# Where in the load order of the second batch's short chunk its single row stands

## The chip, the cores and the metric

The kernel runs on one core of one Trainium2 chip. The metric is the device time of one execution in microseconds; the time of a kernel is the median of its runs. A profiled execution has a time of its own and, inside it, a span, from the first to the last recorded instruction. All positions below ("at 62.1 us") are counted from the start of that span. The engines are PE (matmul), DVE (vector), ACT (scalar), POOL (general purpose) and SP, which here only issues DMAs.

## The reference

```python
X = np.fft.fft(x, axis=1); X = np.fft.fft(X, axis=2); h = X.real       # x: 8 x 3008 x 256, float32
g = h.reshape(24064, 256) @ w_gate                                      # 256 -> 1536
val = h.reshape(24064, 256) @ w_val
out = (g / (1 + exp(-g)) * val) @ w_out                                 # 1536 -> 256
```

For each of eight batches the real part of a two-dimensional Fourier transform is taken over 3008 rows and 256 columns, and a SwiGLU block is applied to each row of it.

## The kernel before

**Transform.** The input rows of a batch are folded by symmetry on POOL (a row with its mirror row, a column with its mirror column), then multiplied on PE with tables of cosines and sines that are made on the chip in the first microseconds. Of the 188 pairs of rows of a folded quarter, 128 form the "long chunk" (tile `XA`, all 128 partitions) and 60 (`NCR`) the "short chunk" (tile `XC`, partitions 0 to 59 or 64 to 123). Row 0 of each quarter has no partner: it is the single row, four rows of 1 KB, put on the partition behind the short chunk (60 or 124).

**The SwiGLU block.** The columns are cut into 24 tiles of up to 512 columns (`wide`); a tile has 12 units of 128 hidden features, so there are 288 units `(t, f)`. A unit makes `g` and `v` on PE (L1336) for the rows and the mirrored rows at once; ACT takes the SiLU (L1448, L1520, L1523), DVE the products (L1539, L1550), and POOL the product of two mirrored units, `hm` (L1547). The pair's operands lie in `sv`, which has two buffers. PE then multiplies `hp` and `hm` with `w_out` (L1598), ACT copies the result out of PSUM (L1604), and SP stores it (L1610). The transform of the next batch (fold on POOL, products at L1756 on PE, sums into `Pt` and `Qt` at L1773 on DVE) runs in between.

**Order.** The first batch's transform and the weights' first part are written out by hand (up to L682). From there all work is recorded as operations with an engine, an estimated duration, reads and writes (`S.add`), and a list scheduler (`Sched.run`) puts them into a fixed order for each engine. For DMAs it models SP's time (`us`), the landing (`lat`) and a shared ring (`ring`). A change of such a number can therefore change the order on every engine. At run time each engine works through its own list in order, waiting on semaphores.

**The loads in question.** `load_c(b)` lists the DMAs of the short chunk: `mid`, the single row (L160); `ups`, 15 DMAs of 32 KB into four partitions each (L158, the rising rows); and the falling sets (L163). For batch 1 the falling sets are split in two halves of four DMAs of 60 KB (`downs[0]`, `downs[1]`, L167), and between the halves a copy inside `XC` (L171) moves one half of the rising rows from partitions 64 to 123 to partitions 0 to 59. `run_loads` hands these DMAs to the scheduler, four to a unit; `k` is the position in the list, and `r` names the earlier positions that the copy reads. Behind them in SP's order come the long chunk of batch 1 (`load_a`: 16 rising DMAs at L148, 4 falling ones of 256 KB at L150), the first stores (L1610), and batch 2's short chunk.

Before all of these SP issues two fills of zeros (L660), 64 KB each, into partitions 60 to 63 and 124 to 127 of `XC`. The single row of batch 1 goes to partition 124, so it has to come after the second fill; the rising and falling rows don't touch those partitions. POOL issues three loads of weights in this time: gate and value columns into `XA` (L387, 512 KB each, at 14.4 and 15.2 us) and `w_out` (L1970, 768 KB, at 24.2 us).

DMAs that SP and ACT issue take eight completion semaphores in turn, so a DMA is issued only when the one eight places earlier has landed.

POOL's list around 62 us reads: `hm` (L1547), `hp` (L1556), the first fold of the long chunk of batch 1 (`SDf<-XA`, L180, and L181), which waits for all of `load_a(1)`, and then `hm` again.

Of the kernel before, what the change touches and what calls it, by code (L numbers as in the profile page):

```python
# [31 lines left out]
def kernel(  # L32
# [33 lines left out]
    NCR = GH - P  # L66
# [50 lines left out]
    XC = const.tile([P, 8, 2, D], F32, name="XC")  # L117
# [14 lines left out]
    LC, NC_ = 4, NCR // 4  # L132

    def up_block(b, j, n):
        return rows_at(b, 2 * j - 1, [[2 * D, n], [R * D, 4], [1, 2 * D]])

    def rows_at(b, row, ap):
        return bass.AP(tensor=x.tensor, offset=(b * M + row) * D, ap=ap)

    def down_set(b, a, j, L, n):  # L140

        return rows_at(b, R * (a + 1) - 2 * j, [[2 * L * D, n], [-2 * D, L], [1, 2 * D]])
# [9 lines left out]
    def load_c(b, q):  # L152

        X3 = XC.rearrange("p a q d -> p a (q d)")
        p0 = 64 * (b % 2)
        pm = p0 + NCR
        r = slice(p0, p0 + NCR)
        ups = [lambda h=h: q.dma_start(out=X3[p0 + LC * h:p0 + LC * (h + 1), 0:4, :],  # L158
                                       in_=up_block(b, JC - LC * h, LC)) for h in range(NC_)]
        mid = [lambda: q.dma_start(out=XC[pm:pm + 1, 0:4, 1],  # L160
                                   in_=rows_at(b, 0, [[R * D, 1], [R * D, 4], [1, D]]))]
        if b != 1:
            return ups + [lambda a=a: q.dma_start(out=X3[r, 4 + a, :], in_=down_set(b, a, JC, LC, NC_))  # L163
                          for a in range(4)] + mid

        def down(a, k):
            q.dma_start(out=XC[0:NCR, 4 + a, 0] if k else XC[r, 4 + a, 0],  # L167
                        in_=rows_at(b, R * (a + 1) - 2 * JC + k, [[2 * LC * D, NC_], [-2 * D, LC], [1, D]]))

        downs = [[lambda a=a, k=k: down(a, k) for a in range(4)] for k in range(2)]  # L170
        return mid + ups + downs[0] + [lambda: q.dma_start(out=XC[0:NCR, 0:4, 1], in_=XC[r, 0:4, 0])] + downs[1]  # L171

    def fold_steps(eng, X, CE, BB, q, r):
        tt = eng.tensor_tensor
# [74 lines left out]
    q = nc.sync  # L249
# [129 lines left out]
    def load_w(first, only=(0, 1)):  # L379
        for i, src in ((0, moe_w_gate), (1, moe_w_val)):  # L380
# [5 lines left out]
            else:  # L386
# [12 lines left out]
                        in_=rows_at(0, 0, [[2 * R * D, 2], [R * D, 2], [1, D]]))  # L399
# [259 lines left out]
    for hi in range(2):  # L659
        q.dma_start(out=X3c[64 * hi + NCR:64 * hi + 64, :].rearrange("p (c d) -> p c d", d=D),  # L660
                    in_=zeros[64 * hi + NCR:64 * hi + 64].unsqueeze(1).to_broadcast([64 - NCR, 16, D]))
# [997 lines left out]
    def run_loads(n):  # L1659
        for what, k, fn in loads[:n]:  # L1660
            up = k < (NA if what[0] == "A" else NC_)
            r, w, us, ring = [], [((what[0],), k)], 0.4 if up else 0.62, 0.57 if up or what[0] == "C" else 1.14
            if what == ("A", 1):
                r = [(("C",), NC_ + 9)]
                us, ring = 0.6, 0.6 if up else 0.9
            if what == ("C", 1):
                us, ring = (0.6, 0.6) if k <= NC_ else (0.9, 0.9)
                if k == NC_ + 5:
                    r = [(("C",), j) for j in range(1, NC_ + 1)]
            S.add("SP", us, fn, r=r, w=w, after=[(("A",), "pre" if k > 15 else "preW")] if what == ("A", 1) else [],  # L1670
                  lat=2.5, ring=ring)
        del loads[:n]
# [4 lines left out]
    def fold_step(what, i, unit):  # L1677
        kind, b = what
        q, j = (1, i) if what == ("C", 1) else divmod(i, 6)
        if i == 0:  # L1680
            run_loads(max((k + 1 for k, (w_, _, _) in enumerate(loads) if w_ == what), default=0))
# [27 lines left out]
    def load_next(what):  # L1709
        kind, b = what  # L1710
        if kind == "A":
            if b + 1 < B:
                loads.extend((("A", b + 1), k, fn) for k, fn in enumerate(load_a(b + 1, nc.sync)))
        else:
            b = b // 2 * 2 + 2
            if b < B:
                loads.extend((("C", b), k, fn) for k, fn in enumerate(load_c(b, nc.sync) + load_c(b + 1, nc.sync)))
# [228 lines left out]
    for i, u in enumerate(units):  # L1946
# [4 lines left out]
        if i == 1:  # L1951
            loads.extend((("C", 1), k, fn) for k, fn in enumerate(load_c(1, nc.sync)))
        if i == A1_LOAD:
            loads[0:0] = ((("A", 1), k, fn) for k, fn in enumerate(load_a(1, nc.sync)))
        run_loads(LOADS if i < 20 else LOADS_LATER)
        if i in ROW_PE:
            row_op(ROW_PE[i])
# [7 lines left out]
        if i == RESCALE:  # L1965
            state["scaled"] = True
            S.add("ACT", 1.3, lambda: nc.scalar.activation(Wm[:, 1], Wm[:, 1], AF.Copy, scale=-0.5),
                  r=[(("Wm",), (fc, 1)) for fc in range(3)], w=[(("Wm",), 1)])
# [58 lines left out]
```

## Time and profile before

| | |
|---|---|
| time, median of 3 runs | 607.42 us (605.87 to 609.76) |
| time of the profiled execution | 608.12 us |
| its span | 606.3 us |
| mean granted TensorE clock | 0.997 |
| busy share of the span: PE, DVE, ACT, POOL | 98%, 94%, 93%, 84% |
| data moved by DMA | 57.65 MB, 95 GB/s on average |

A busy share is an average over the whole span; PE's matmuls are pipelined, so that its busy time counts overlaps once. Waits are inferred from semaphores: a wait for several of them is put down to the one that came last, and sometimes to a neighbour of it.

### The profile page before, as it was taken

Reading aid. Unit: us, or ns where it says so; the run is one execution under the profiler, and the core shown is the slowest. Engines: PE = TensorE matmul, PEld = TensorE weight load, DVE = VectorE, ACT = ScalarE, POOL = GpSimd, SP = SyncE. Lnnn points to the kernel's source line nnn. Section 1 sums busy time; section 2 is a strip of 40 time slices with the busy share of each in tenths; the row PEclk is TensorE's granted clock in tenths of the full one; section 3 lists DMA queues with packets and bytes.
Section 4 is the critical chain, followed back from the end, with each engine's and each line's share of the span. In section 5 each row is a group of like instructions: output and inputs, shape, how many; then the busy total and the mean of one; then the engine's idle time right before and its main releaser. Section 6 shows DMA issues by size and latency. Waiting matters only on the chain.

```text
span 606.3 us, 12501 instructions
## 1 busy us (share of the span) xinstructions
PE 592.3 (98%) x3974; PEld 391.8 (65%) x4031; DVE 572.3 (94%) x1055; ACT 562.1 (93%) x1086; POOL 509.7 (84%) x460
## 2 busy tenths in 40 slices
PE   8999799999999999999999999999999999999997
PEld 5456566666666666666666666666666666666686
DVE  8989799999999999999999999999999999999993
ACT  8899797899989899999999999999999999999994
POOL 8717999999899999998999988888878467687772
PEclk9999899999999999999999999999999999999999
DMA  9837347354725514454234212037211112111112
GB/s 240 124 99 136 113 125 158 104 135 115 159 71 114 129 53 124 119 134 123 62 100 120 70 45 81 18 87 186 63 62 37 55 45 62 45 54 51 54 53 78
DMA packets 50554, 57.65 MB, mean 95 GB/s; under 512 B 7267, under 2 KB 37399, under 8 KB 50489
## 3 DMA queue, kind: packets, MB, share of 16 engines
q1 hardware_dynamic: 47529, 53.97, 33.4%
q0 software_dynamic: 2672, 2.36, 2.6%
q8 instruction: 31, 0.51, 0.3%
q10 hardware_dynamic: 288, 0.52, 0.3%
q14 instruction: 34, 0.28, 0.2%
HBM read 29.43 MB, written 24.65 MB: 89 GB/s over the span
## 4 chain that ended last, share of the span: by engine, by line
PE 82%; DMA 6%; DVE 4%; SPq 2%; ACT 2%; issue 2%; POOL 1%; ACTq 0%; DVEq 0%
PE o L1598 37%; PE g L1336 22%; PE v L1336 18%; DMA XC<-in_x_dram 2%; PE g L1756 2%; DMA XA<-in_x_dram 2%; PE o L1756 2%; DMA XC<-Af 1%; DVE sv L1539 1%; SPq L167 1%; DMA out_dram<-ev 1%; PE v L1598 1%; DVE hp L1550 1%; POOL EOA L502 0%; DVE SA L444 0%
## 5 line engine op out<-in xcount | busy, mean ns | idle before, releaser
L1547 POOL TENSOR_TENSOR hm<-sv 128x1024 bf16<-128x1024 f32 (+2 forms) x137 | 254.9, 1862 | 51.1 <-ACT sv L1523 23.2
L1539 DVE SCALAR_TENSOR_TENSOR sv<-es,v 128x512 f32<-128x512 f32 (+2 forms) x264 | 175.6, 669 | 9.5 <-PE v L1336 4.5
L1598 PE MATMUL o<-Wo,hm 128*128 128x256 bf16 (+1 forms) x1128 | 164.6, 273 | 0.5
L1550 DVE TENSOR_TENSOR hp<-sp,v 128x512 bf16<-128x512 f32 (+2 forms) x238 | 157.7, 670 | 4.7 <-PE v L1336 3.8
L1598 PE MATMUL o<-Wo,hp 128*128 128x256 bf16 (+1 forms) x1104 | 159.9, 272 | 0.7
L1598 PEld LDWEIGHTS <-hm 128*128 128x128 bf16 (+2 forms) x1140 | 112.2, 99 | 59.4 <-issue 3.3
L1598 PEld LDWEIGHTS <-hp 128*128 128x128 bf16 (+2 forms) x1140 | 111.9, 98 | 54.6 <-issue 1.8
L1523 ACT ACTIVATE sv<-g 128x512 f32<-128x512 f32 (+2 forms) x182 | 121.3, 681 | 6.2 <-POOL hm L1547 3.1
L1448 ACT ACTIVATE sp<-g 128x512 f32<-128x512 f32 (+2 forms) x182 | 113.2, 626 | 6.3 <-PE g L1336 3.8
L1336 PE MATMUL g<-Pt,Wp 128*128 128x512 bf16 (+2 forms) x281 | 105.4, 375 | 4.0 <-ACT sv L1523 2.9
L1409 ACT ACTIVATE v<-bc,w 128x512 f32<-128x512 bf16 (+2 forms) x146 | 105.7, 726 | 2.0 <-DVE sv L1539 1.0
L1336 PE MATMUL v<-Pt,Wp 128*128 128x512 bf16 (+2 forms) x287 | 105.3, 375 | 0.4
L1471 ACT ACTIVATE es<-v 128x512 f32<-128x512 f32 (+2 forms) x146 | 90.7, 623 | 5.9 <-DVE sv L1539 3.2
L1473 DVE SCALAR_TENSOR_TENSOR es<-bc,w,v 128x512 f32<-128x512 bf16 (+2 forms) x128 | 93.2, 732 | 2.8 <-PE v L1336 0.4
L1336 PE MATMUL g<-Qt,Wq 128*128 128x512 bf16 (+2 forms) x249 | 91.5, 375 | 0.4
L1336 PEld LDWEIGHTS <-Wp 128*128 128x128 bf16 x576 | 56.3, 98 | 26.7 <-issue 1.6
L1336 PE MATMUL g<-Qt,Wm 128*128 128x512 bf16 (+2 forms) x192 | 72.1, 377 | 0.4
L1452 DVE SCALAR_TENSOR_TENSOR sg<-bc,w,g 128x512 f32<-128x512 bf16 (+2 forms) x92 | 66.1, 721 | 1.4 <-PE g L1336 1.0
L1523 ACT ACTIVATE sv<-sg 128x512 f32<-128x512 f32 (+2 forms) x92 | 64.0, 699 | 1.0 <-DVE sg L1516 0.9
L1336 PEld LDWEIGHTS <-Wq 128*128 128x128 bf16 x430 | 42.0, 98 | 31.5 <-issue 7.1
L1520 ACT ACTIVATE sp<-g 128x512 f32<-128x512 f32 (+2 forms) x92 | 56.9, 619 | 5.5 <-DVE sg L1516 5.1
L1516 DVE SCALAR_TENSOR_TENSOR sg<-sg,g 128x512 f32<-128x512 f32 (+2 forms) x92 | 60.7, 660 | 0.3 <-PE g L1336 0.2
(196 smaller groups left out, 769.9 us busy)
## 6 DMA issues: line engine op xcount, KB each, us to landing
out_dram<-ev SPq DMA_DIRECT2D x96, 128.0 KB
XA<-in_x_dram SPq DMA_DIRECT2D x30, 256.0 KB
XA<-in_x_dram SPq DMA_DIRECT2D x112, 64.0 KB
XC<-in_x_dram SPq DMA_DIRECT2D x28, 120.0 KB
XC<-in_x_dram SPq DMA_DIRECT2D x105, 32.0 KB
bc<-br SPq DMA_DIRECT2D x19, 128.0 KB
St<-Fc SPq DMA_DIRECT2D x12, 128.5 KB
out_dram<-ev SPq DMA_DIRECT2D x12, 120.0 KB
```

Source lines behind the costliest of these rows:

```text
L1336: nc.tensor.matmul(ps[:, :n], Wt[:, gv, fs], src[:, :n], start=start, stop=stop, skip_group_check=True)
L1409: nc.scalar.activation(T_[kv][:, :w], bc[t][:, :w], AF.Copy, scale=w0[:, 1, f:f + 1])
L1448: nc.scalar.activation(sp_to()[:, :w], T_[kg][:, :w], AF.Silu)
L1452: nc.vector.scalar_tensor_tensor(T_[keg][:, :w], bc[t][:, :w], w0[:, 0, f:f + 1], T_[kg][:, :w], op0=Alu.mult, op1=Alu.add)
L1471: nc.scalar.activation(T_[kes][:, :w], T_[kv][:, :w], AF.Copy, scale=2.0 if on_pool(u) > 1 else 1.0)
L1473: nc.vector.scalar_tensor_tensor(T_[kes][:, :w], bc[t][:, :w], w0[:, 1, f:f + 1], T_[kv][:, :w], op0=Alu.mult, op1=Alu.add)
L1516: nc.vector.scalar_tensor_tensor(T_[kgm][:, :w], T_[keg][:, :w], 2.0, T_[kg][:, :w], op0=Alu.mult, op1=Alu.subtract)
L1523: nc.scalar.activation(sv()[:, f % 2, w - 1::-1, 1], T_[kgm if by_dve else kg][:, :w], AF.Silu)
L1539: nc.vector.scalar_tensor_tensor(sv()[:, f % 2, w - 1::-1, 0], T_[kes][:, :w], 2.0, T_[kv][:, :w], op0=Alu.mult, op1=Alu.subtract)
L1547: nc.gpsimd.tensor_tensor(hts_(t)[1][:, f - 1:f + 1, :w], sv()[:, :, :w, 1], sv()[:, :, :w, 0], op=Alu.mult)
L1550: nc.vector.tensor_tensor(hts_(t)[0][:, f, :wp], T_[ksp][:, :wp], T_[kv][:, :wp], op=Alu.mult)
L1598: nc.tensor.matmul(st["ps"][:n, j, :], hts[t][minus][:, f, c:c + n], Wo[:, f, :], start=(f == 0), stop=(f == nF - 1))
```

## The change

The DMA of the single row of batch 1 moves from the head of the list to the place behind `downs[0]`, directly ahead of the copy. The list keeps 25 DMAs. In `run_loads` the numbers follow: the rising rows are now positions 0 to 14, and the single row, now position 19, gets the scheduler's costs of the falling sets (0.9 us) in place of those of the rising rows (0.6 us).

```diff
-        return mid + ups + downs[0] + [lambda: q.dma_start(out=XC[0:NCR, 0:4, 1], in_=XC[r, 0:4, 0])] + downs[1]
+        return ups + downs[0] + mid + [lambda: q.dma_start(out=XC[0:NCR, 0:4, 1], in_=XC[r, 0:4, 0])] + downs[1]
...
             if what == ("C", 1):
-                us, ring = (0.6, 0.6) if k <= NC_ else (0.9, 0.9)
+                us, ring = (0.6, 0.6) if k < NC_ else (0.9, 0.9)
                 if k == NC_ + 5:
-                    r = [(("C",), j) for j in range(1, NC_ + 1)]
+                    r = [(("C",), j) for j in range(NC_)]
```

In the compiled order, the lists of all engines are the same up to the place that runs at about 66 us before the change. There one pair changes places on DVE (`hp`, L1550, now ahead of `sv`, L1539). From about 82 to 160 us neighbouring instructions change places on PE (219 places of its list), DVE (32), ACT (26) and POOL (8), and one pair on SP; behind 160 us the lists are the same again. The number of instructions stays.

## The prediction

> **What bounds the kernel now.** I read the busy shares first. PE is busy nearly all the time, so time is lost only where PE stands still or its clock drops.
>
> ```profile
> PE 592.3 (98%) x3974; PEld 391.8 (65%) x4031; DVE 572.3 (94%) x1055; ACT 562.1 (93%) x1086; POOL 509.7 (84%) x460
> ```
>
> Next came busy time by stretches, to find where PE stands still (columns: stretch, length, busy time of PE, PEld, DVE, ACT, POOL with counts, granted clock, DMA share, GB/s).
>
> ```profile
> 64.20:67.20 3.00, 0.06 (x2) 0.04 (x1) 0.73 (x2) 0.64 (x1) 3.00 (x4) 0.91 0.45 140
> 67.20:70.60 3.40, 3.40 (x14) 2.01 (x14) 3.29 (x6) 3.24 (x7) 3.40 (x4) 0.58 0.40 106
> ...
> 76.00:160.00 84.00, 82.86 (x562) 55.24 (x567) 80.71 (x153) 74.43 (x147) 82.28 (x80) 1.00 0.49 127
> ```
>
> PE is empty for 3 us at 64.2, and the next 3.4 us run at a mean clock of 0.58, which costs another 3.4 x 0.42 = 1.4 us. From 76 to 160 us it lacks 1.1 us in all. The waits between 62 and 76 us say who is behind the hole:
>
> ```profile
> POOL SDf L180 <- DMA out_dram<-ev: 5.1, 1, 5.1
> DVE sv L1539 <- POOL hm L1547: 4.0, 1, 4.0
> ...
> ACT sv L1523 <- POOL hm L1547: 3.1, 1, 3.1
> PE g L1336 <- ACT sv L1523: 2.9, 1, 2.9
> ```
>
> POOL's fold waits 5.1 us, `hm` stands behind it, ACT and DVE need the `sv` buffer that `hm` frees, and PE needs the `g` bank that ACT frees. The fold's releaser is named as a store, but the fold waits for the loads into `XA`; the store was merely issued behind them. POOL's list confirms the order:
>
> ```profile
> 62.08 2.35 POOL L180 TENSOR_TENSOR SDf<-XA 128x1020 f32<-128x1020 f32 x1 [5.05 <-DMA out_dram<-ev]
> 64.39 0.21 POOL L181 TENSOR_TENSOR EOf<-XA 128x4 f32<-128x4 f32 x1
> 64.54 1.89 POOL L1547 TENSOR_TENSOR hm<-sv 128x1024 bf16<-128x1024 f32 x1
> ```
>
> So these loads set the hole, and what is issued ahead of them on SP matters:
>
> ```profile
> 16.58 1.49 SPq L660 DMA_DIRECT2D XC<-Af  x2
> 26.11 0.64 SPq L160 DMA_DIRECT2D XC<-in_x_dram  x1
> 26.80 8.16 SPq L158 DMA_DIRECT2D XC<-in_x_dram  x15
> 35.16 3.62 SPq L167 DMA_DIRECT2D XC<-in_x_dram  x4
> 38.97 0.89 SPq L171 DMA_DIRECT2D XC<-XC  x1
> 39.90 3.49 SPq L167 DMA_DIRECT2D XC<-in_x_dram  x4
> 43.56 0.68 SPq L148 DMA_DIRECT2D XA<-in_x_dram  x2
> ```
>
> SP stands for 8.0 us (18.1 to 26.1) until the second zero fill has landed, because the single row writes the same partition. From 35.2 us on it issues without a pause until the `XA` loads begin at 43.56.
>
> **The change, part by part.**
>
> *The wait.* The rising rows don't touch the filled partitions, so SP may issue them at 18.1 us. But DMAs take eight semaphores in turn: the first six rising rows find theirs free, the seventh needs the first fill's, the eighth the second fill's. Thus six of 15 are issued by 20.3 us (0.34 us each, the spacing of L148), the seventh after the first fill, the eighth at 26.1 as the single row was. The 8 us wait mostly moves to the seventh and eighth rising row. All 25 DMAs remain.
>
> *What the early six gain.* The view of DMA queues in two stretches (q1 is SP's queue, q0 POOL's) decides:
>
> ```profile
> q0 software_dynamic: 394, 0.77, 105.3%
> ...
> q0 software_dynamic: 1257, 0.64, 120.2%
> ```
>
> The first is 16.6 to 20.8 us, the second 26.0 to 30.2 us. In neither did one packet of q1 start, though the fills (issued 16.6) and then the single row and seven rising rows (issued 26.1 to 29.0) were waiting: POOL's weight loads, then `w_out`, kept SP's queue out. Between them the fills drain until about 25.2 us. So the early rows, queued behind the fills, have some 0.8 us before `w_out` starts at 26.0. Their pace: the single row landed at 31.06 (the next issue on its semaphore is at 31.08) and the eighth rising row at 35.15 (which released L167 at 35.16), so 4.09 / 8 = 0.51 us a row. That is 0.8 / 0.51, hence one to two rows done, and one more takes the single row's first turn at 30.2: two to three rows, 1.0 to 1.5 us. I take 1.3. The first falling set, which waits for the eighth rising row, goes out at 33.9 instead of 35.16. Bounds: nothing gets through early (0), or the early rows run beside `w_out` (below, 3.3).
>
> The Trainium skill, page "DMA: Bandwidth & Descriptors", section "Queues, rings and completion order", says that a DMA engine goes round between queues, a packet of at most 64 descriptors at a time. Taken as a fair share this speaks for the larger gain; the trace, with no q1 packet in 4.2 us twice, shows a far coarser turn. By the rule the first falling set would go out near 31.9, by the rows at 33.9.
>
> *The single row in its new place.* It stands between the fourth falling set and the copy: 0.64 us plus a gap of 0.05, 0.69 us, now in the stretch where SP issues without pause. Behind it are the copy, four falling sets, and all loads into `XA`. Before, it lay ahead of them too, but there the rows' landings, not SP, set the pace. Its own waits are over by then. Net: 1.3 - 0.7 = 0.6 us earlier for the `XA` loads (43.0).
>
> *On to PE.* The loads move as a block, so the fold starts at 61.5 and `hm` at 63.9; the hole shrinks from 2.9 to 2.3 us. No drop of the clock followed the 0.8 us that PE stood at 10.4, one followed 2.9 us; 2.3 is nearer to the latter, so I leave the 1.4 us in. Gain 0.6. Nothing is gained beyond POOL's lead: it is busy without a pause from 62.1 to 93.9 us, and PE's transform at 91.08 uses a fold that ends at 90.44, 0.6 us of slack.
>
> The Trainium skill, page "TensorE: Matmul & The Clock Gate", section "Part 1: The HAM clock gate", puts the fall at an idle window of about 3.4 us; here 2.9 us was enough. By that rule 2.3 us would not lower the clock, and the sum would be up to 0.6 us better, what POOL's slack allows.
>
> *The scheduler.* The single row's cost in the model rises by 0.3 us, and the lists between 82 and 160 us change. The swap at 66 us is harmless: `hp` may run in the hole. The others have no price in the trace. From below: the one PE wait between 76 and 160 us, 0.66 us at 145.8 (PE for ACT), goes away. From above: a hole like the one at 64 us with its slow clock, 2.9 + 1.4 = 4.3. Since the swapped instructions are neighbours, I price them by the 0.66 us row, half a chance of one more: +0.3.
>
> *Sum.* -0.6 + 0.3 = -0.3 us on the profiled execution (608.12, span 606.3). It lies 0.7 above the median, 607.42; I apply the difference to the median: 607.1.
>
> **The rivals.**
>
> *A, the early rows run beside `w_out`.* With half of the engines' time from 26.0, 1.6 rows are through by then, 5.1 more by 31.2, the eighth at 31.9: 3.3 us earlier, 2.6 after the single row's cost. The hole and the slow clock vanish, but POOL's lead of 2.6 plus at most 0.6 of slack caps the gain: 3.0, so 604.4. For it: between 20.8 and 23 us both queues had packets (128 and 46). Against: the two empty stretches.
>
> *B, the single row now costs its 0.69 us.* If the fills drain later because the early rows crowd them, no row gets through before `w_out`, and the `XA` loads, the fold and PE's hole move out by 0.7: 608.1. It decides when less than 1.4 rows are through by 26.0. For it: the fills' slow drain (the DMA share from 23.0 to 26.1 is 0.14). This is slower, though within 1%.
>
> *C, the new order opens a hole.* One between 82 and 160 us costs 4.3 as at 64 us, two 8.6: 611.4 to 616. Against: the swaps are small. For: PE there has only 1.1 us to lose and the other engines are at 89 to 98%, so a late buffer is not absorbed. It decides from some 3 us of lateness.
>
> *D, the change does nothing:* SP waits for the fills anyway at the seventh row. It is the forecast with 0 in place of 0.6 and shares its chance.
>
> **How the numbers follow.** Forecast (with D) 0.52, A 0.22, B 0.13, C 0.13. Its own range is 606.0 to 608.0. For the whole, low is the full removal of the hole and clock loss (607.4 - 4.3 = 603.1), a little lower for the scatter of a median; high takes in B and part of C: 602.8 to 610.3. A measurement of this kernel can tell about 1%, 6 us, from no change. Over 1% faster needs more than the hole holds, so only A with scatter: 0.05. Over 1% slower needs two holes of C or one very long: 0.10. The rest, 0.85, lies within.
>
> **What would show it.** Six L158 issues from 18.1, a wait of SP at the seventh and eighth until about 26.1, L167 near 33.9, L160 behind four of them, the first L148 at 43.0, POOL's L180 at 61.5, PE's hole at 64 near 2.3 us. I am wrong if L148 starts before 41.5 (A) or after 43.6 (B), or if PE waits over 2 us between 82 and 160 us (C).

## The result and the profile after

The changed kernel takes 604.2 us (median of 9 runs, 603.54 to 605.0), the kernel before, timed beside it, 608.3 us (9 runs, 605.82 to 611.05): a ratio of 0.9931, 95% interval 0.9909 to 0.9954. That is 0.7% faster. The profiled execution took 604.29 us with a span of 602.4 us (before 608.12 and 606.3). Single executions of one kernel lie up to 8 us apart here, so verdicts go by timed medians, and a profile is one draw. The page's busy shares of the changed kernel look as before:

```profile
PE 591.5 (98%) x3974; PEld 392.1 (65%) x4031; DVE 572.8 (95%) x1055; ACT 562.6 (93%) x1086; POOL 509.4 (85%) x460
```

PE's busy time falls by only 0.8 us, though the span is 3.9 us shorter. The stretches around 64 us tell more (stretch, length, busy time of PE, PEld, DVE, ACT, POOL with counts, granted clock, DMA share, GB/s):

```profile
63.50:66.50 3.00, 2.46 (x17) 1.54 (x16) 2.50 (x4) 2.47 (x5) 3.00 (x3) 1.00 0.41 115
66.50:70.00 3.50, 3.44 (x25) 2.18 (x23) 3.50 (x7) 3.50 (x9) 3.50 (x4) 1.00 0.56 155
76.00:160.00 84.00, 82.86 (x560) 55.14 (x566) 81.29 (x153) 75.59 (x148) 82.17 (x78) 1.00 0.50 132
```

The hole of 2.9 us is down to 0.5, and no stretch at half clock follows: the clock is 1.00 where it was 0.58. These two are the gain: 2.4 us of hole and 1.4 us of slow clock, 3.8 of the 3.9 us. From 76 to 160 us PE is busy for 82.86 us, to the hundredth as before, although its list changed there. The waits from 50 to 90 us of the changed kernel show the same chain as before, each link shorter:

```profile
POOL SDf L180 <- DMA out_dram<-ev: 4.5, 1, 4.5
...
DVE sv L1539 <- POOL hm L1547: 1.0, 1, 1.0
ACT sv L1523 <- POOL hm L1547: 0.7, 1, 0.7
...
PE g L1336 <- ACT sv L1523: 0.5, 1, 0.5
```

POOL's own list of the changed kernel puts the fold 2.6 us earlier (62.08 before), and `hm` too (64.54 before):

```profile
59.49 2.35 POOL L180 TENSOR_TENSOR SDf<-XA 128x1020 f32<-128x1020 f32 x1 [4.51 <-DMA out_dram<-ev]
61.81 0.20 POOL L181 TENSOR_TENSOR EOf<-XA 128x4 f32<-128x4 f32 x1
61.97 1.89 POOL L1547 TENSOR_TENSOR hm<-sv 128x1024 bf16<-128x1024 f32 x1
```

SP's issues in the changed kernel say where it comes from:

```profile
16.62 1.49 SPq L660 DMA_DIRECT2D XC<-Af  x2
18.15 11.56 SPq L158 DMA_DIRECT2D XC<-in_x_dram  x15
32.20 3.61 SPq L167 DMA_DIRECT2D XC<-in_x_dram  x4
35.86 0.65 SPq L160 DMA_DIRECT2D XC<-in_x_dram  x1
36.62 0.89 SPq L171 DMA_DIRECT2D XC<-XC  x1
37.55 3.94 SPq L167 DMA_DIRECT2D XC<-in_x_dram  x4
41.67 2.38 SPq L148 DMA_DIRECT2D XA<-in_x_dram  x7
```

The 15th rising row has been issued by 29.71. With eight semaphores in turn that needs the seventh row landed: so seven rows are in `XC` before 29.7 us, where before the first of them landed only after 31 us. The first falling set goes out 2.96 us earlier (32.20 for 35.16), the loads into `XA` 1.89 us earlier (41.67 for 43.56). The difference is the single row (0.76 us from its issue to the copy's) and 0.46 us more for the second falling half, less 0.15 in the first half.

In the DMA queues of the changed kernel from 26.0 to 30.2 us (packets, MB, share of 16 engines), SP's queue is no longer absent:

```profile
q0 software_dynamic: 1201, 0.61, 115.3%
q1 hardware_dynamic: 100, 0.16, 11.5%
```

Of these 100 packets 89 start between 26 and 28 us, beside `w_out`. SP's queue (q1) from 24 to 26 us and then POOL's (q0) from 26 to 28 us in the kernel before, where SP's has no packet in that second stretch:

```profile
q1 hardware_dynamic: 28, 0.03, 7.7%
q0 software_dynamic: 426, 0.22, 94.6%
```

SP's queue from 24 to 26 us and both queues from 26 to 28 us in the changed kernel:

```profile
q1 hardware_dynamic: 73, 0.10, 27.0%
q0 software_dynamic: 376, 0.19, 87.3%
q1 hardware_dynamic: 89, 0.15, 20.9%
```

### The profile page after: what moved, and what is told of

Its sections match the earlier page's. It is cut to its first block, busy times and chain, and to the rows that moved or that the text cites. A ratio compares the mean times of both kernels' runs of the same rounds, so it can differ in the third digit from the quotient of the medians.

```text
span 602.4 us, 12497 instructions
## 1 busy us (share of the span) xinstructions
PE 591.5 (98%) x3974; PEld 392.1 (65%) x4031; DVE 572.8 (95%) x1055; ACT 562.6 (93%) x1086; POOL 509.4 (85%) x460
## 4 chain that ended last, share of the span: by engine, by line
PE 81%; DMA 6%; DVE 4%; ACT 3%; POOL 2%; issue 2%; SPq 2%; POOLq 0%; ACTq 0%; DVEq 0%
PE o L1598 36%; PE g L1336 22%; PE v L1336 18%; PE g L1756 2%; DMA XC<-in_x_dram 2%; PE o L1756 2%; DMA XC<-Af 2%; DVE sv L1539 1%; DMA XA<-in_x_dram 1%; SPq L167 1%; DMA out_dram<-ev 1%; PE v L1598 1%; DVE hp L1550 1%; ACT sp L1448 1%; ACT v L1409 1%
## 5 line engine op out<-in xcount | busy, mean ns | idle before, releaser
L1539 DVE SCALAR_TENSOR_TENSOR sv<-es,v 128x512 f32<-128x512 f32 (+2 forms) x264 | 176.1, 672 | 5.9 <-PE v L1336 4.2
L1550 DVE TENSOR_TENSOR hp<-sp,v 128x512 bf16<-128x512 f32 (+2 forms) x238 | 158.1, 672 | 4.4 <-PE v L1336 3.8
```

Source lines behind the costliest of these rows:

```text
L1539: nc.vector.scalar_tensor_tensor(sv()[:, f % 2, w - 1::-1, 0], T_[kes][:, :w], 2.0, T_[kv][:, :w], op0=Alu.mult, op1=Alu.subtract)
L1550: nc.vector.tensor_tensor(hts_(t)[0][:, f, :wp], T_[ksp][:, :wp], T_[kv][:, :wp], op=Alu.mult)
```

## The experiments

The theory: SP's rows get through before `w_out` only if they are queued ahead of it; this brings the `XA` loads, and so POOL's fold, forward until PE hardly waits. The first rival: the gain is due to the new lists between 66 and 160 us. The second: `w_out` alone, as the block, sets the start of the `XA` loads. The kernel before was timed beside each group of four experiments, each group on another chip; its medians were 607.55 (35 runs, first four kernels), 609.33 (35, next four) and 609.38 us (26, last four). The ratios below compare with these runs.

**The loads and the lists apart.** The changed DMA order with the old cost for the single row, which gives the old lists on all computing engines:

```diff
-                us, ring = (0.6, 0.6) if k < NC_ else (0.9, 0.9)
+                us, ring = (0.6, 0.6) if k < NC_ or k == NC_ + 4 else (0.9, 0.9)
```

> The loads stand as in the change, but the scheduler's cost of the single row is put back to 0.6 us, so that the lists of PE, DVE, ACT and POOL are those of before, place by place. Theory 1 (the early rising rows let the loads into XA begin earlier, PE's hole at 64 us and the slow clock behind it go): time ratio to before 0.992 to 0.995, first L148 near 41.7 us, hole below 0.8 us, no half clock. Theory 2 (the new order of the compute lists brings the gain): ratio 0.998 to 1.002.

Measured: 605.49 us, ratio 0.9968 [0.9946, 0.9990], between the ranges of the two theories. The first L148 came at 41.53 us as expected, but the profile has a hole of 2.9 us with half clock, which theory 1 had excluded. Run again with the last group:

> The first experiment once more (early rows, lists of before), to tell its 0.9968 from the 0.9931 and 0.9941 of the changed kernel. Theory 1 (the early rows alone bring it all): ratio 0.992 to 0.9955. Theory 2 (the lists bring a part, once the rows are early): ratio 0.9955 to 0.999.

Measured: 606.77 us, 0.9960 [0.9934, 0.9986], in the range of theory 2, though the interval reaches into that of theory 1. The old DMA order with the new cost, hence the new lists:

```diff
-                us, ring = (0.6, 0.6) if k <= NC_ else (0.9, 0.9)
+                us, ring = (0.6, 0.6) if 0 < k <= NC_ else (0.9, 0.9)
```

> The loads stand as before the change, but the single row costs 0.9 us in the scheduler's model, so that the lists of PE, DVE, ACT and POOL are those of the changed kernel. Theory 1: hole of 2.3 to 3 us at 64 us with the slow clock, first L148 at 43.5, ratio 0.998 to 1.003. Theory 2: ratio 0.992 to 0.995 and no hole.

Measured: 607.23 us, 0.9997 [0.9971, 1.0022], the time of theory 1; the one profile, with a hole of 0.8 us, is not what it expected. The moved load alone brings a gain, the lists alone none that shows. The changed kernel again:

> The changed kernel itself, beside the next three on the same chip. Theory 1 (the time is set by when the loads into XA have landed; the start of these loads is now 1.9 us earlier): ratio 0.992 to 0.996. Theory 2 (the new compute lists add to the early rows; the early rows alone gave 0.9968): ratio below 0.995, clearly under the kernel of the first experiment.

Measured: 604.42 us, 0.9941 [0.9914, 0.9968], which fits both theories. The moved load with the old lists has kept some 0.4%, the whole change 0.6 to 0.7%. The intervals overlap; whether the lists add 0.2% once the loads come early stays open.

The profiles of these runs need care. In the waits of the second kernel (old loads, new lists) the fold is late by little, although its loads began at 43.20 us:

```profile
POOL SDf L180 <- DMA XA<-in_x_dram: 3.2, 1, 3.2
...
PE g L1336 <- ACT sv L1523: 0.8, 1, 0.8
```

That execution took 605.02 us, among the fastest of its kernel: its `XA` loads took 16.4 us from the first issue to the fold, those of the first kernel's profile 20.3, with the same lists until then. The next table sorts that out.

**What the time follows.** Each row is one profiled execution: first issue into `XA`, time from it to the fold, start of the fold (L180), PE's hole at 64 us, whether half clock followed, and the execution's time in us.

| kernel | first L148 | loads took | fold | hole | half clock | time |
|---|---|---|---|---|---|---|
| changed, `w_out` late | 37.68 | 17.1 | 54.76 | 0 | no | 603.85 |
| changed, again | 41.22 | 16.2 | 57.37 | 0 | no | 602.96 |
| single row behind six | 41.60 | 17.7 | 59.27 | 0.39 | no | 605.11 |
| changed | 41.67 | 17.8 | 59.49 | 0.54 | no | 604.29 |
| old loads, new lists | 43.20 | 16.4 | 59.64 | 0.79 | no | 605.02 |
| changed, 6 spare loads | 43.87 | 16.3 | 60.20 | 0.82 | no | 604.60 |
| new loads, old lists, again | 41.53 | 19.2 | 60.72 | 2.09 | yes | 607.50 |
| new loads, old lists | 41.53 | 20.3 | 61.82 | 2.91 | yes | 608.24 |
| before | 43.56 | 18.5 | 62.08 | 2.94 | yes | 608.12 |
| old loads, new lists, 6 spare | 44.90 | 17.5 | 62.37 | 3.74 | no | 606.76 |
| before, `w_out` late | 44.05 | 18.9 | 62.93 | 3.01 | yes | 609.66 |
| changed, 24 spare loads | 48.72 | 19.3 | 68.03 | 9.02 | yes | 614.14 |

The fold's start decides: up to 57.4 us there is no hole, from 59.3 on there is one, mostly the longer the later the fold, and half clock comes with five of the six longest. In these single executions a fold at 54.8 gains nothing over one at 57.4. The two kernels with all rows early (below) are left out: their folds, at 58.98 and 58.84 us, waited for nothing, because PE and with it POOL had been held up before. The loads' own time scatters by 4 us between executions and moves the fold as much as the change does; the change shifts the start of all of them by 1.9 us.

The mean granted clock of every timed execution adds to these single profiles. One half-clock stretch of 3.4 us takes 0.003 off the mean over a span, as in the profile before (0.997); half clock at the very end of the program takes at most 0.0015 off in the profiles. A mean of 0.997 or less was found in 60 of 96 executions of the kernel before, in 7 of 12 with the old loads and new lists, in 1 of 21 of the changed kernel, and in 7 of 36 of the three kernels with early rows and old lists. So the early rows remove the half clock from most executions. Of the executions above 0.997, those of the changed kernel have a median of 604.2 us and those of the kernel before 606.0, so some 2 us of the gain remain where no half clock at 64 us takes part.

**Only the early rows.** From the kernel before, with old lists: the single row goes behind the first six rising rows, which alone found free semaphores.

```diff
-        return mid + ups + downs[0] + [lambda: q.dma_start(out=XC[0:NCR, 0:4, 1], in_=XC[r, 0:4, 0])] + downs[1]
+        return ups[:6] + mid + ups[6:] + downs[0] + [lambda: q.dma_start(out=XC[0:NCR, 0:4, 1], in_=XC[r, 0:4, 0])] + downs[1]
...
-                    r = [(("C",), j) for j in range(1, NC_ + 1)]
+                    r = [(("C",), j) for j in range(NC_ + 1) if j != 6]
```

> The single row stands behind the first six rising rows, in front of the other nine; compute lists as before the change. Theory 1: six rows pass before w_out's stream, one less than in the change (the seventh went out at 24.95 there); first L148 at 41.5 to 42.5, ratio 0.992 to 0.996. Rival (it matters that the single row stands behind the falling sets, for instance because it holds a semaphore that later rows need): hole over 2 us, ratio 0.998 to 1.002.

Measured: 605.18 us, 0.9956 [0.9933, 0.9979], as theory 1 expected. SP's list of this kernel:

```profile
18.06 3.42 SPq L158 DMA_DIRECT2D XC<-in_x_dram  x6
25.83 0.66 SPq L160 DMA_DIRECT2D XC<-in_x_dram  x1
26.54 6.29 SPq L158 DMA_DIRECT2D XC<-in_x_dram  x9
33.22 3.61 SPq L167 DMA_DIRECT2D XC<-in_x_dram  x4
...
41.60 2.39 SPq L148 DMA_DIRECT2D XA<-in_x_dram  x7
```

Here too SP waits until 25.8 for the fill, and `XA` starts at 41.60, as in the changed kernel. So removing the wait is not what gains. Six rows queued ahead of `w_out` bring it, wherever the single row then stands.

**`w_out` later.** In the kernel before, its DMA is issued at 29.3 us instead of 24.2; the scheduler's entry stays.

```diff
+                if (fc, gv) == (2, 0):
+                    nc.gpsimd.dma_start(out=Wo, in_=moe_w_out.rearrange("(f p) d -> p f d", p=P))
...
-            S.add("POOL", 1.06, lambda: nc.gpsimd.dma_start(out=Wo, in_=moe_w_out.rearrange("(f p) d -> p f d", p=P)),
+            S.add("POOL", 1.06, lambda: None,
```

> The kernel before, except that w_out is issued some 5.7 us later on POOL (behind the third L1819, near 29.9 us instead of 24.2). The single row stays first and SP still waits for the fill until 26.1. Theory 1 with its blocked queue: the rising rows then meet an idle queue, the eighth lands near 29.5 instead of 35.15, the first falling set goes out at 29.5 to 31, first L148 at 38 to 40, no hole, ratio 0.991 to 0.995. Rival (the 8 us wait of SP is itself the cost, the stream of w_out is not): first L148 stays at 43 to 43.6, hole 2.9, ratio 0.998 to 1.002.

Measured: 607.72 us, 1.0008 [0.9979, 1.0037]: a miss for theory 1, and for the second rival. Time and hole (3.0 us) are those that the expectation gave to SP's wait as the cost; but the six early rows gained with that wait in place, so the wait does not explain them. SP's list of this kernel does:

```profile
26.52 6.43 SPq L158 DMA_DIRECT2D XC<-in_x_dram  x15
32.99 4.38 SPq L167 DMA_DIRECT2D XC<-in_x_dram  x4
39.46 0.89 SPq L171 DMA_DIRECT2D XC<-XC  x1
...
44.05 4.22 SPq L148 DMA_DIRECT2D XA<-in_x_dram  x10
```

The first falling set comes 2.2 us earlier than before, but the copy 0.5 us later: `w_out` now holds up the last rows and the falling sets. The block only moved. With both, `w_out` late in the changed kernel:

> The changed kernel with w_out issued behind the third L1819, so that all 15 rising rows pass before it and it meets the falling sets instead. Theory 1: falling sets from 29.5 us, first L148 at 37.5 to 39.5, L180 on XA at 54 to 58, no hole, ratio 0.990 to 0.994, the best of all. Rival (w_out's stream now holds the copy or lands behind PE's first use at 40.7): first L148 not before 41, or a wait of PE there of over 0.5 us, ratio 0.994 to 1.000.

Measured: 603.69 us (6 runs), 0.9908 [0.9873, 0.9944], as theory 1 expected; the lowest median of all, though its interval overlaps that of the changed kernel. POOL's list of it:

```profile
54.76 2.36 POOL L180 TENSOR_TENSOR SDf<-XA 128x1020 f32<-128x1020 f32 x1 [0.26 <-DMA XC<-in_x_dram]
```

The fold waits 0.26 us, not 4.5: with the early rows already through, there is less for `w_out` to hold up. The loads no longer bound this place, so what is left to gain here is small.

**All rows early.** In the changed kernel the two fills go behind the 14th and 15th rising row, so that SP waits for neither of them; once with the new lists, once (with the first experiment's line) with the old.

```diff
+        for i in range(2):
+            ups[NC_ - 2 + i] = lambda i=i, up=ups[NC_ - 2 + i]: (up(), fill(i))
...
-    for hi in range(2):
+    def fill(hi):
```

> The changed kernel with the two zero fills of the spare partitions moved behind the 14th and 15th rising row, so that all rising rows can go out before w_out and none waits for a fill. Theory 1: first L148 at 35 to 39 us, POOL's L180 on XA at 54 to 58, no hole at 64 and no slow clock in any run, ratio 0.989 to 0.994. Rival (the early rows crowd the weight loads that PE needs from 17 to 26 us): PE stands for 1 us or more between 16 and 30 us, ratio 0.995 to 1.002.

> The same with the single row's cost at 0.6 us in the model, so that the lists of PE, DVE, ACT and POOL are those of before. Theory 1: as the run before, ratio 0.989 to 0.994, since with the loads early enough the order of the lists has nothing left to give. Theory 2 (the lists themselves gain): ratio at least 0.003 above that of the run before.

Measured: 608.28 us, 0.9994 [0.9965, 1.0022], and 608.46 us, 1.0009 [0.9981, 1.0037]: theory 1 missed in both, the rival of the first came, and the lists show no gain. The rows go out from 9.4 us and `XA` starts at 35.87, 5.8 us earlier than in the changed kernel, yet nothing is gained. In the new-lists kernel the waits from 15 to 30 us have a new line, and the stretches show its price:

```profile
PE o L466 <- DMA W<-in_moe_w_val_dram: 3.8, 1, 3.8
```

```profile
16.90:20.80 3.90, 0.12 (x2) 0.07 (x1) 1.48 (x7) 0.18 (x1) 3.80 (x7) 1.00 1.12 211
20.80:24.60 3.80, 3.80 (x20) 2.13 (x20) 0.15 (x1) 2.03 (x4) 1.88 (x3) 0.56 0.47 99
```

Now POOL's second load into `W` comes late beside SP's rows: 9.4 us from issue to landing, 4.1 before. PE stands for 3.8 us at 17 us and then runs at half clock; the hole at 64 is gone, and the two about cancel (span 606.6 us, before 606.3). So the delay works in both directions: POOL's loads hold up SP's rows, and SP's rows hold up POOL's loads.

**Delay at the end of the chain.** Six, then 24 loads of 128 bytes into a tile that nobody reads, on SP directly ahead of the `XA` loads, in the changed kernel (24 in place of 6 in the second; L148 is L149 in these kernels, L180 L188):

```diff
+    spare = const.tile([P, 32], F32, name="spare")
...
+        def spare_loads(last=downs[1][3]):
+            last()
+            for j in range(6):
+                q.dma_start(out=spare[j:j + 1], in_=rows_at(1, j, [[D, 1], [1, 32]]))
+
+        downs[1][3] = spare_loads
```

> The changed kernel with six small extra loads (128 bytes each, into a tile that nothing reads) between the short chunk and the loads into XA: some 3.6 us of SP's time. Theory 1: first L148 at 45 to 46, L180 on XA at 62.5 to 64.5, hole of 3 to 5 us with the slow clock, ratio 0.999 to 1.006. Rival (the start of the XA loads doesn't set PE's hole): ratio 0.992 to 0.996 as the changed kernel.

Measured: 604.33 us, 0.9934 [0.9905, 0.9964], beside 604.42 without them: a miss for theory 1, and the ratio that its rival gave. They moved the first L148 by 2.2 us, to 43.87, but no cost shows.

> The changed kernel with 24 instead of six spare loads ahead of the loads into XA (0.31 us each in the six of before, so some 7.5 us). Theory 1: first L148 at 48.5 to 50.5 us, L180 on XA at 65 to 69, PE's hole 5.5 to 9 us with the slow clock, ratio 1.003 to 1.012. Rival (the start of the XA loads doesn't set the time, as six spare loads seemed to say): ratio 0.992 to 0.996.

Measured: 614.19 us, 1.0087 [1.0059, 1.0116], as theory 1 expected. Waits from 50 to 80 us of this kernel:

```profile
POOL SDf L188 <- DMA out_dram<-ev: 13.2, 1, 13.2
...
PE g L1344 <- ACT sv L1531: 9.0, 1, 9.0
```

`XA` starts 7.05 us later than in the changed kernel, the hole is 8.5 us longer, and the time rises by 9.8 us over 604.42, slow clock included. So the start of these loads does set the time once the delay is long. The six in the old DMA order with the new lists:

> The kernel of the second experiment (single row first, new lists; 0.9997) with the six spare loads. If the early rising rows are what gained with six spare loads: first L148 at 45 to 46, ratio 0.999 to 1.006. Rival (the spare loads themselves gain, because SP's queue drains before the loads into XA begin, or because the spare tile shifts other tiles): ratio 0.992 to 0.996.

Measured: 607.76 us, 0.9975 [0.9945, 1.0005], beside 0.9997 without them, between the two ranges. No clear cost here either, and no clear gain, so the spare loads do not replace the early rows. Why 2.2 us cost nothing is not settled. In the single trace of the six the last `XA` issue was only 1.1 us later than in the changed kernel (53.51 for 52.44), so half of the delay was regained there; without the early rows it was not (55.02 for 53.33).

## Why the prediction was right in part, and the step that failed

The forecast was 607.1 us, 0.3 below the 607.42 of the kernel before; measured were 604.2 us, 4.1 below its new median of 608.3. The direction and the place were right, the size was not.

- **Place of the loss and chain of waits: right.** In the two profiles the hole at 64 us and its slow clock are 3.8 of the 3.9 us gained, and the table ties the hole to the fold's start.
- **Six rows early, the wait moves on: right.** Six issues from 18.15, the eighth at 26.56 (26.1 forecast).
- **"Two to three rows", 1.3 us: this step failed.** It gave the rows 0.8 us, from the end of the fills to the start of `w_out`. Seven rows got through, and the first falling set went out at 32.20, not 33.9. Of them some two were through by 26.0 us (SP's queue moved 0.20 MB from 20.8 to 26 us, 0.13 of it the fills), close to the forecast's one to two. The other five ran from 26.0 to 30.2 us beside `w_out` (0.16 MB), where the forecast had none, and one at 30.2. The pace was right: beyond the 0.03 MB that SP's queue moved before in these two stretches, it now moved 0.10 + 0.15 - 0.03 = 0.22 MB from 24 to 28 us, 6.9 rows of 32 KB, or 0.58 us a row (0.51 forecast). The time was wrong, 4 us and not 0.8. I read the empty stretch of before as "`w_out` keeps SP's queue out". It kept out what was issued at 26.1 us or later; what had been queued before it (six rows since 18 us, the seventh at 24.95) ran on beside it. Why the earlier ones get through, no run shows. Nor is the split fixed: with six early rows SP's queue moved 0.15 MB from 24 to 26 us and only 0.05 from 26 to 28 us.
- **The rule weighed against it.** By the rule of the Trainium skill that a DMA engine goes round between queues (page "DMA: Bandwidth & Descriptors", section "Queues, rings and completion order") the falling set would have gone out near 31.9; 32.20 was measured, so the rule was nearer than my reading, but by another course. From 26 to 28 us SP's queue moved 0.15 MB and POOL's 0.19, close to a fair share in bytes, though not in packets (89 and 376); from 28.0 to 30.2 us SP's queue started 11 packets and POOL's 825, far from one.
- **Single row 0.69 us: right,** 0.76. The `XA` loads gained 1.89 us (0.6 forecast), and in this profile took 0.7 us less.
- **Hole 2.3 us with its slow clock: wrong, as what follows from that step.** With the fold at 59.49 for 61.5, the hole is 0.5 us and the 1.4 us of slow clock are gone. To leave the slow clock in at 2.3 us was sound: in another kernel a hole of 2.09 us brought it.
- **Scheduler +0.3 us: nothing shows.** The 0.66 us wait of PE moved from 145.8 to 142.2 us; lists alone, 0.9997. Rival C did not come.
- **Rival A's mechanism came, its cap did not hold.** Rows ran beside `w_out`, and the slow clock and nearly all of the hole went. Its sum is off: 2.6 + 0.6 is 3.2, not 3.0. The two profiles differ by 3.9 us, more than this cap by POOL's lead. POOL runs 2.6 to 2.7 us earlier up to 92 us, then 3.8, because a wait for DVE that ended at 94.93 us before (first line) is gone in the changed kernel (second line):

```profile
94.93 1.89 POOL L1547 TENSOR_TENSOR hm<-sv 128x1024 bf16<-128x1024 f32 x1 [1.05 <-DVE sv L1539]
91.13 1.89 POOL L1547 TENSOR_TENSOR hm<-sv 128x1024 bf16<-128x1024 f32 x1
```

That 604.4 us still lies beside the measured 604.2 is in part luck: it was reckoned from 607.42, and the kernel before came to 608.3 when timed again.

- **Rivals B and D did not come.** B needed fewer than 1.4 rows ahead of `w_out`, and D a fold that stays.

## What to carry to other kernels

When the engine that issues DMAs stands at a wait and a large transfer of another queue is about to start, put independent small transfers ahead of the wait: what counted here is which was queued first, not how long the issuing engine waited. Do not push them ahead of a load that a busy engine needs soon; here PE then stood for 3.8 us in another place. Judge it by medians where a transfer's own duration scatters as much as the change moves its start.

## What the runs showed of the hardware that was not expected

**The clock does not go by the length of the hole alone.** The new loads with old lists (run again) had a hole of 2.09 us, from 63.71 to 65.80, and half clock behind it. The old loads with new lists and six spare loads had a hole of 3.74 us, from 63.71 to 67.44, and none. The traces' records of the clock say why. In each profile all changes of the clock lie a whole number of 3.413 us apart; in the kernel before the clock rises first at 5.19 us, falls at 66.63, 18 such windows later, and rises at 70.05. Cut into these windows, the two kernels read (stretch, length, busy time of PE, granted clock, DMA share, GB/s):

```profile
63.64:67.06 3.42, 1.27 (x8) 1.00 0.41 117
67.06:70.47 3.41, 3.41 (x14) 0.50 0.47 129
```

```profile
62.20:65.61 3.41, 1.50 (x11) 1.00 0.27 94
65.61:69.03 3.42, 1.59 (x9) 1.00 0.43 125
69.03:72.44 3.41, 3.35 (x25) 1.00 0.41 133
```

The shorter hole lies inside one window, in which PE stands for 63%; the longer one is divided between two, with 56% and 54%. In the windows of all fourteen profiles half clock followed each in which PE stood for 63% or more, and none in which it stood for 56% or less. So the window runs on by itself and is judged at its end. The Trainium skill, page "TensorE: Matmul & The Clock Gate", section "Part 1: The HAM clock gate", calls its window of 3413 ns free-running; these profiles agree with both. Whether a hole of some 2 to 4 us brings the slow clock is then a matter of phase too, and part of the scatter between executions.

**The same loads into `XA` took 16.2 to 20.3 us** from the first issue to the fold in the twelve executions of the table. In the five executions with old lists the mean is 18.9 us, in the seven with new lists 17.2, although the lists are equal until 66 us; with so few draws this may be chance, and its cause is open.
